# Converting all fourteen weight units of a GLU's second pass during attention, and five first loads of them at once

## The chip, the cores and the metric

The kernel runs on one core of a Trainium2 chip. The metric is the device time of one execution in microseconds (us); lower is better. The engines are named as in the profile: PE (matmuls) with PEld (its weight loads), DVE (VectorE), ACT (ScalarE), POOL (GpSimd) and SP (SyncE, which issues most DMA transfers, in the order of its queue).

## The reference

Random-feature attention over 8 batches, 8 heads, 576 tokens and head dimension 64, with 128 features; its output, as 4608 tokens by 512 features, goes through a gated linear unit with 1536 hidden columns.

```python
def phi(x):                      # x scaled by 64 ** -0.25
    h = einsum('bhsd,md->bhsm', x, omega) - sum(x * x, -1) / 2
    return exp(h - max(h, -1)) / sqrt(m)
q_p, k_p = phi(q_s), phi(k_s)
kv, z = einsum('bhsm,bhsd->bhmd', k_p, v), sum(k_p, 2)
attn = einsum('bhsm,bhmd->bhsd', q_p, kv) / (einsum('bhsm,bhm->bhs', q_p, z)[..., None] + 1e-6)
x = attn.transpose(0, 2, 1, 3).reshape(4608, 512)
out = (1 / (1 + exp(-(x @ w_gate))) * (x @ w_val)) @ w_out
```

The three weight matrices come as 64-bit floats, and the kernel itself turns their bits into 32-bit floats.

## The kernel before, in words

Every product of the gated unit is made of three fp32r matmuls: an operand is split into a high part (a copy on ACT) and a low part (a subtraction on DVE or POOL), and low times high, high times low and high times high are added in PSUM.

**Attention and the first pass.** `attention` is a generator over many small tasks (norms, keys, queries). Its results go to a DRAM tensor `xT`, whose tokens become ready in chunks of 512 (9 chunks). `first_pass` (the generator `gates`) makes 4 of the 12 hidden column tiles for each chunk as soon as its tokens are ready: it loads `xr`, splits it into `xe` (L71, L72), and for each column tile makes a gate and a value product of 12 matmuls (L245) into PSUM. ACT applies Tanh to the gate (`ge`, L266), DVE multiplies (`ye`, L273), SP stores `ye` to DRAM (L278). Each product is one step of `gates`: 8 a chunk, 72 in all. `g` and `y` have two buffers each. The loop that runs attention takes one step of `gates`, then 19 or 11 of attention, and so on until all tokens are ready; what is left of the 72 steps comes after it, when attention's memory (the pool `a`) has been given back to a pool `late`.

**Weights.** The first pass's weights (8 column tiles `wh`, `wl`) are converted at the start. The rest are 14 *units*: eight for the gate and value columns of the second pass, six for the output product. `convert_weights` loads a unit's 64-bit words into a tile (L142, two loads of 512 KB), turns each half into 32-bit floats with six DVE instructions and one on POOL (`from_float64`, L79 to L97), adds four sums of blocks on POOL (L178), and stores the 1 MB result to the DRAM tensor `w32` (L179). It is a generator too: a call issues the loads, a second and a third convert a half each, and the sums and the store come at the beginning of the next call, which goes on to the next unit. Before, 11 units are converted during attention, in two tiles of pool `a` tagged `cv` (the profile's `c`), one call to each step of `gates` from the tenth on (`FROM`); the last 3 (`N_TAIL`) are converted after attention in three of the five `u` buffers of pool `late` (the profile's `late`).

**Units in use.** `unit` loads seven of a unit's eight blocks (L197, L198; 384 and 512 KB) into a `u` tile, and on its second call splits it into high and low parts (L212, L213). There are five `u` buffers in `late` (`UL`) and three in `tail` (`UE`), a pool in the memory that the first pass's weights give back when it is over.

**The second pass** makes the other 8 column tiles: for each of the 9 chunks, `operands` loads `xr` again and makes seven combinations of its blocks (`xl`, `s`; L291, L294, L298), and 8 groups (`gated`) of seven products of six matmuls (L349) follow, group g with unit g. `unit` calls for units not yet split are taken one to a group. The operands of the first chunk are made during the last eight steps of the first pass. Then the output product is made (`last`, L463) and stored.

**Order.** Instructions written with `pin` keep their program order; the others are placed in their engine's queue by a scheduler before the kernel runs. Each engine's queue then runs in order.

Of the kernel before, what the change touches and what calls it, by code (L numbers as in the profile page):

```python
# [14 lines left out]
U32 = mybir.dt.uint32  # L15
# [5 lines left out]
P = 128  # L21
# [14 lines left out]
Q = NC // 2  # L36
# [7 lines left out]
N_LATE = 2 * (NPAIR - EP) + NPAIR  # L44
# [1 line left out]
AT_ONCE = 6  # L46
AHEAD = 8
EVERY = 8
FROM = 10
N_TAIL = 3  # L50
RATE = 11
FIRST = 19

# [4 lines left out]
UL, UE = 5, 3  # L58
# [7 lines left out]
N_OPS = 7  # L66
# [34 lines left out]
def attn_glu_kernel(ctx: ExitStack, tc, qT, kT, qn, kn, va, om, ident, w, out):  # L101
# [610 lines left out]
    def ready(n):  # L712

        return all(through[p] * P >= n for p in range(NP))

    keep = ctx.enter_context(tc.tile_pool(name="keep", bufs=1))
    late = None
    stores = []
    with tc.tile_pool(name="early", bufs=1) as early:
        gates = first_pass()  # L720
        with tc.tile_pool(name="a", bufs=1, side="right") as pool:
            steps = attention(pool)

            def tiles(name):
                return pool.tile([P, 7 * WP], U32, tag="cv", bufs=2, name=name)

            conv = first_weights(early, tiles)
            cycle[:] = ["at", "at", "at", "gv"]
            n = 0
            while not ready(NC):  # L730
                next(steps, None)
                n += 1
                if n % EVERY == 0:
                    next(conv, None)
            cycle.clear()
            later = convert_weights(tiles, range(N_LATE - N_TAIL))
            n = credit = 0
            while not ready(B * S):
                next(gates)
                credit += RATE if n >= 2 * NE - 2 else FIRST  # L740
                while credit >= 1 and not ready(B * S):
                    next(steps, None)
                    credit -= 1
                n += 1
                if next(conv, conv) is conv and n >= FROM:
                    next(later, None)
            for _ in later:
                pass
        late = ctx.enter_context(tc.tile_pool(name="late", bufs=1, side="right"))
        cycle[:] = ["at", "at", "at", "gv"]  # L750

        def tiles(name):
            u = late.tile([P, 2, N_OPS, Q], U32, tag="u", bufs=UL, name=name)
            return u.rearrange("p i n q -> p (i n q)")


        left = 2 * NE * NCH - n
        started, later, parts = [], iter(()), iter(())
        for n, _ in enumerate(gates):
            if n == 2:  # L760
                free = [tiles(f"late{i}") for i in range(N_TAIL)]
                later = convert_weights(lambda name: free.pop(0), range(N_LATE - N_TAIL, N_LATE))
                started = [unit(late, n) for n in range(2)]
                for one in started:
                    next(one)
            elif n in (3, 4):
                next(started[n - 3])
            next(later, None)
            if n == left - 2 * NE:
                parts = operands(0)  # L770
                x = next(parts)
            elif n > left - 2 * NE:
                next(parts, None)
        assert not free and next(later, later) is later
        started = [unit(late, n) for n in range(2, UL)]
        for one in started:
            next(one)

    tail = ctx.enter_context(tc.tile_pool(name="tail", bufs=1))
    started += [unit(tail, n) for n in range(UL, UL + UE)]  # L780
    for one in started[UL - 2 :]:
        next(one)
    next(started.pop(0))
    raws = []
    for c, pair, kind in second_pass(x, parts):
        g = 2 * (pair - EP) + kind
# [99 lines left out]
```

## Time and profile before

| | us |
|---|---|
| median of 3 runs | 1259.02 (1257.65 to 1262.58) |
| the profiled execution's own time | 1265.94 |
| its span, first to last instruction | 1264.1 |
| PE busy | 1199.4 (95% of the span) |
| DVE, ACT, POOL busy | 844.1, 470.4, 425.4 |
| mean granted TensorE clock | 0.961 of full speed |

The profiled execution lies above the three runs; the profile is used for where time goes, the median for the time itself. The stages follow each other roughly so: attention with most of the first pass to about 531 us, the rest of the first pass to about 604, the second pass to about 984, the output product to the end. In a row of the order of time stand the start, the duration, the engine, the line and the operation, and in square brackets the engine's idle time before it and what ended that. A row of windows gives the window, its length, then busy time and count of PE, PEld, DVE, ACT and POOL, the granted clock, the DMA engines' busy share and GB/s.

### The profile page before, as it was taken

How to read it: one execution, taken by the hardware profiler on the slowest of the kernel's cores; microseconds unless marked ns; L12 is line 12 of the kernel's file. 1: busy time of each engine (PE TensorE's matmuls, PEld its weight loads, DVE VectorE, ACT ScalarE, POOL GpSimd, SP SyncE). 2: the span in 40 equal slices, each digit the busy share in tenths (PEclk: the TensorE clock that was granted, in tenths of full speed). 3: DMA queues.
4: the chain of work that ended last, by engine and by line, in shares of the span. 5: the costliest groups of instructions: out<-in, count | busy, mean ns of one | idle time of the engine just before them, and what ended most of it. 6: DMA issues, size and time to landing. Idle time of an engine off the chain costs nothing.

```text
span 1264.1 us, 23448 instructions
## 1 busy us (share of the span) xinstructions
PE 1199.4 (95%) x8956; PEld 1108.8 (88%) x8956; DVE 844.1 (67%) x1838; ACT 470.4 (37%) x963; POOL 425.4 (34%) x435
## 2 busy tenths in 40 slices
PE   5989899999999999999799999999999899999998
PEld 4878778788778787778699999999998899999998
DVE  5654758878777667364866565665668787666774
ACT  3325344445434343230622222322224444333331
POOL 2130010413133122055276666666666211111110
PEclk9978979999989898799799999999999999999999
DMA  8455455668666671265623433233328675666553
GB/s 276 149 173 164 127 165 177 230 217 269 239 201 202 211 243 60 71 231 208 208 88 122 151 122 118 92 122 123 137 83 282 208 219 190 196 192 199 187 184 109
DMA packets 99185, 219.38 MB, mean 174 GB/s; under 512 B 10496, under 2 KB 31232, under 8 KB 97280
## 3 DMA queue, kind: packets, MB, share of 16 engines
q1 hardware_dynamic: 86832, 198.94, 47.6%
q10 hardware_dynamic: 12240, 18.95, 4.1%
q8 instruction: 70, 1.15, 0.4%
q14 instruction: 43, 0.35, 0.1%
HBM read 141.82 MB, written 76.02 MB: 172 GB/s over the span
## 4 chain that ended last, share of the span: by engine, by line
PE 45%; DVE 5%; DMA 3%; issue 1%; SPq 1%; POOL 1%; ACT 0%; DVEq 0%; POOLq 0%; ACTq 0%
PE gw L349 25%; PE po L463 20%; DMA u<-w 1%; DMA xr<-xT 1%; DVE u L213 1%; DMA yr<-ye 1%; POOL late L97 1%; DVE yl L72 0%; DVE late L89 0%; DVE yr L454 0%; DMA ye<-ye 0%; POOL late L178 0%; DVE late L79 0%; DVE late L82 0%; DVE s L298 0%
## 5 line engine op out<-in xcount | busy, mean ns | idle before, releaser
L349 PE MATMUL gw<-xl,u 128*128 128x256 f32 x3024 | 366.0, 283 | 12.3 <-ACT xl L291 4.6
L349 PEld LDWEIGHTS gw<-xl,u 128*128 128x128 f32 x3024 | 363.7, 191 | 14.6 <-ACT xl L291 5.2
L463 PE MATMUL po<-u,yh 128*128 128x256 f32 x1512 | 272.4, 283 | 0.0
L463 PEld LDWEIGHTS po<-u,yh 128*128 128x128 f32 x1512 | 234.8, 191 | 0.0
L463 PE MATMUL po<-u,yl 128*128 128x256 f32 x756 | 214.0, 283 | 4.3 <-DVE yl L72 4.3
L245 PE MATMUL gv<-xe,wh 128*128 128x512 f32 x576 | 194.3, 412 | 1.5 <-POOL xe L72 1.4
L71 ACT ACTIVATE yh<-yr 128x896 fp32r<-128x896 f32 x108 | 99.1, 948 | 159.7 <-DVE yr L454 48.6
L463 PEld LDWEIGHTS po<-u,yl 128*128 128x128 f32 x756 | 144.3, 191 | 4.9 <-DVE yl L72 4.9
L245 PEld LDWEIGHTS gv<-xe,wh 128*128 128x128 f32 x576 | 110.1, 195 | 24.6 <-POOL xe L72 3.6
L245 PE MATMUL gv<-xe,wl 128*128 128x512 f32 x288 | 120.6, 420 | 1.1 <-ACT xe L71 1.1
L72 POOL TENSOR_TENSOR xe<-xr,xe 128x512 fp32r<-128x512 f32 x36 | 48.7, 1371 | 206.5 <-ACT xe L71 203.0
L72 POOL TENSOR_TENSOR yl<-yr,yh 128x896 fp32r<-128x896 f32 x17 | 36.2, 2129 | 218.1 <-ACT yh L71 141.2
L72 DVE TENSOR_TENSOR yl<-yr,yh 128x896 fp32r<-128x896 f32 x91 | 97.2, 1100 | 13.0 <-ACT yh L71 12.0
L594 PE MATMUL pkv<-v,kp 128*128 128x66 f32 x512 | 91.1, 307 | 13.1 <-ACT kp L584 13.1
L594 PEld LDWEIGHTS pkv<-v,kp 128*128 128x128 f32 x512 | 81.3, 221 | 24.0 <-ACT kp L584 17.6
L454 DVE TENSOR_TENSOR yr<-yr 128x128 f32<-128x128 f32 x144 | 60.9, 456 | 60.0 <-DMA yr<-ye 59.5
L329 DVE TENSOR_TENSOR u<-gw,p 128x256 f32<-128x256 f32 x144 | 60.6, 421 | 60.0 <-PE gw L349 50.7
L97 POOL TENSOR_TENSOR c<-c 128x512 f32<-128x512 f32 x22 | 28.1, 1276 | 158.9 <-DVE c L95 88.0
L584 ACT ACTIVATE kp<-ppk,nb 128x128 f32<-128x128 f32 x256 | 69.7, 389 | 30.9 <-DVE nb L575 24.9
L646 PE MATMUL pn<-kv,qp 128*128 128x66 f32 (+1 forms) x640 | 79.4, 279 | 0.0
L646 PEld LDWEIGHTS pn<-kv,qp 128*128 128x128 f32 (+1 forms) x640 | 73.4, 194 | 5.2 <-ACT qp L635 1.9
L635 ACT ACTIVATE qp<-pt 128x512 f32<-128x512 f32 (+1 forms) x80 | 43.6, 554 | 86.8 <-PE pt L633 80.3
(106 smaller groups left out, 1774.6 us busy)
## 6 DMA issues: line engine op xcount, KB each, us to landing
yl<-yl SPq DMA_DIRECT2D x36, 896.0 KB, 3.9
yr<-yl SPq DMA_DIRECT2D x72, 448.0 KB, 4.0
xr<-xT SPq DMA_DIRECT2D x72, 256.0 KB, 4.2
c<-w SPq DMA_DIRECT2D x22, 512.0 KB, 4.6
w<-c SPq DMA_DIRECT2D x11, 1024.0 KB, 4.8
v<-va SPq DMA_DIRECT2D x32, 330.0 KB, 3.7
natk<-kn SPq DMA_DIRECT2D x36, 256.0 KB, 3.6
natq<-qn SPq DMA_DIRECT2D x36, 256.0 KB, 3.3
```

The lines of the kernel that those rows point to most:

```text
L71: nc.scalar.activation(out=hi, in_=x, func=AF.Copy)
L72: (lo_engine or nc.vector).tensor_tensor(out=lo, in0=x, in1=hi.bitcast(F32), op=ALU.subtract)
L97: nc.gpsimd.tensor_tensor(out=x, in0=x, in1=r, op=ALU.add)
L245: nc.tensor.matmul(gv, lhsT=u[:, s], rhs=v, start=(m == 0), stop=(m == 3 * KC - 1))
L329: return nc.vector.tensor_tensor(out=o, in0=a, in1=b, op=ALU.add)
L349: nc.tensor.matmul(o, lhsT=u[:, k, s], rhs=v[:, kc, :], start=(first and m == 0), stop=(m == 5), skip_group_check=not first,)
L454: nc.vector.tensor_tensor(out=raw[:, o], in0=raw[:, a], in1=raw[:, b], op=op)
L463: nc.tensor.matmul(o, lhsT=u[:, i, :], rhs=v[:, k, :], start=(j + m == 0 and n in (1, 6, 5, 4)), stop=(j == NPAIR - 1 and m == 2), skip_gr ...
L584: nc.scalar.activation(out=kp[t, h], in_=pp[:, i, :], func=AF.Exp, bias=nb[:, t - t0, h : h + 1], scale=SCALE,)
L594: nc.tensor.matmul(pkv[:, h, :], lhsT=kp[b * MID + i, h], rhs=v[:, i, h, :], start=(i == 0), stop=(i == MID),)
L635: nc.scalar.activation(out=qp, in_=pt, func=AF.Exp)
L646: nc.tensor.matmul(pn[r, i, :], lhsT=qp[:, i, r], rhs=kvs[u, p, bb][:, h, :], start=True, stop=True,)
```

## The change

All 14 units are converted during attention, in the `cv` tiles, one call to each step of `gates` from the fourth on. After attention no unit is converted: all five `u` buffers of `late` go to units 0 to 4, whose loads are issued together on step 2, and which are split on steps 3, 6, 9, 12 and 15. Units 5 to 7 are loaded when the first pass is over, as before, and split one to a group from the first group on. Before, units 0 and 1 were loaded on step 2 and split on steps 3 and 4, and units 2 to 4 were loaded when the first pass was over.

```diff
@@ -46,8 +46,7 @@
 AT_ONCE = 6
 AHEAD = 8
 EVERY = 8
-FROM = 10
-N_TAIL = 3
+FROM = 4
 RATE = 11
 FIRST = 19
@@ -733,7 +732,7 @@
             cycle.clear()
-            later = convert_weights(tiles, range(N_LATE - N_TAIL))
+            later = convert_weights(tiles, range(N_LATE))
             n = credit = 0
             while not ready(B * S):
                 next(gates)
@@ -749,38 +748,26 @@
         late = ctx.enter_context(tc.tile_pool(name="late", bufs=1, side="right"))
         cycle[:] = ["at", "at", "at", "gv"]
-        def tiles(name):
-            u = late.tile([P, 2, N_OPS, Q], U32, tag="u", bufs=UL, name=name)
-            return u.rearrange("p i n q -> p (i n q)")
-
-
         left = 2 * NE * NCH - n
-        started, later, parts = [], iter(()), iter(())
+        started, parts = [], iter(())
         for n, _ in enumerate(gates):
             if n == 2:
-                free = [tiles(f"late{i}") for i in range(N_TAIL)]
-                later = convert_weights(lambda name: free.pop(0), range(N_LATE - N_TAIL, N_LATE))
-                started = [unit(late, n) for n in range(2)]
+                started = [unit(late, n) for n in range(UL)]
                 for one in started:
                     next(one)
-            elif n in (3, 4):
-                next(started[n - 3])
-            next(later, None)
+            elif started and n % 3 == 0:
+                next(started.pop(0))
             if n == left - 2 * NE:
                 parts = operands(0)
                 x = next(parts)
             elif n > left - 2 * NE:
                 next(parts, None)
-        assert not free and next(later, later) is later
-        started = [unit(late, n) for n in range(2, UL)]
-        for one in started:
-            next(one)
+        assert not started
     tail = ctx.enter_context(tc.tile_pool(name="tail", bufs=1))
-    started += [unit(tail, n) for n in range(UL, UL + UE)]
-    for one in started[UL - 2 :]:
+    started = [unit(tail, n) for n in range(UL, UL + UE)]
+    for one in started:
         next(one)
-    next(started.pop(0))
     raws = []
     for c, pair, kind in second_pass(x, parts):
```

## The prediction

> **What bounds the kernel now.** I read the page first (busy shares, the 40 slices, the chain that ended last), then the windows by stage, then the order of time around the one slice where PE drops.
>
> ```profile
> span 1264.1 us, 23448 instructions
> PE 1199.4 (95%) x8956; PEld 1108.8 (88%) x8956; DVE 844.1 (67%) x1838; ACT 470.4 (37%) x963; POOL 425.4 (34%) x435
> PE   5989899999999999999799999999999899999998
> PEclk9978979999989898799799999999999999999999
> 102.00:194.00 92.00, 85.16 (x624) 72.35 (x624) 53.91 (x144) 42.49 (x124) 5.04 (x4) 0.89 0.50 150
> 194.00:500.00 306.00, 293.34 (x2127) 247.63 (x2125) 231.92 (x592) 135.35 (x353) 82.22 (x83) 0.96 0.62 205
> 500.00:531.00 31.00, 27.95 (x202) 24.25 (x200) 17.87 (x56) 8.60 (x16) 0.00 (x0) 0.85 0.22 82
> 531.00:604.00 73.00, 72.03 (x306) 58.17 (x304) 38.51 (x52) 19.22 (x30) 33.28 (x30) 0.97 0.65 225
> ```
>
> The window rows give length, then busy time (and count) of PE, PEld, DVE, ACT, POOL, then granted clock, DMA share and GB/s. PE is the bound nearly everywhere: 293.34 of 306 us in the middle of attention, 72.03 of 73 in the end of the first pass. A change to DVE and POOL work can only pay where PE waits. The slice string of PE has one clear dip in the middle (the "7", slice 20, 600 to 632 us), and PEclk has its "7" there too. In order of time, PE's own rows there are:
>
> ```profile
> 603.40 0.61 PE L245 MATMUL gv<-xe,wh 128*128 128x512 f32 x2
> 603.95 0.39 PE L349 MATMUL gw<-xl,u 128*128 128x256 f32 x1
> 605.38 0.86 PE L349 MATMUL gw<-xl,u 128*128 128x256 f32 x5 [1.04 <-POOL xl L294]
> 610.87 0.58 PE L349 MATMUL gw<-xl,u 128*128 128x256 f32 x1 [4.64 <-ACT xl L291]
> 613.15 2.72 PE L349 MATMUL gw<-xl,u 128*128 128x256 f32 x11 [1.70 <-DVE xl L294]
> 617.38 15.96 PE L349 MATMUL gw<-xl,u 128*128 128x256 f32 x120 [1.51 <-ACT p L360]
> 608.00:620.00 12.00, 5.92 (x24) 5.33 (x25) 9.62 (x13) 5.33 (x10) 2.87 (x2) 0.50 0.45 135
> ```
>
> The first pass ends at 603.9 (L245) and the second pass (L349) starts haltingly: idle 1.04 + 4.64 + 1.70 + 1.51 = 8.9 us for operands of its first chunk, and half clock (0.50) from 608 to 620. Why the operands are late:
>
> ```profile
> 589.68 0.32 SPq L179 DMA_DIRECT2D w<-late  x1
> 590.10 0.38 SPq L278 DMA_DIRECT2D ye<-ye  x1
> 590.52 2.21 SPq L222 DMA_DIRECT2D xr<-xT  x2
> 593.32 0.50 SPq L197 DMA_DIRECT2D u<-w  x1
> 595.26 0.69 DVE L273 SCALAR_TENSOR_TENSOR ye<-ge,gv 128x512 f32<-128x512 f32 x1 [8.81 <-DMA ye<-ye]
> 599.83 0.85 ACT L212 ACTIVATE u<-u 128x768 fp32r<-128x768 f32 x1 [13.29 <-DMA u<-w]
> ```
>
> SP issues in order. The store of the third late unit (L179) can go only at 589.68, when POOL has finished its sums; behind it stood a store of ye, half of the operand load xr and the loads of units 2 to 4. So DVE waited 8.81 us for a free y, ACT 13.29 us for a unit, and the operands' splits and sums, queued behind those in order, ran until 617. All of it goes back to the three units converted in this stage.
>
> **What the change moves.** Counted from the loops, attention's loop makes 46 of the 72 steps of the first pass (70 attention steps come before; then 19 attention steps to each of the first six, 11 to each later one), which leaves 26; the 306 matmuls of the 531:604 row are 25.5 products of 12, which fits. The generator of the first weights is empty at step 1. Before, calls to the converter fell on steps 10 to 46: 37 calls, and 11 units take 34 (three each and one to end); the last one's store, on step 43, went at 499.31 (last row below). After, they fall on 4 to 46: 43 calls, exactly what 14 units take. Unit i is then loaded on step 4+3i, converted on the next two, summed and stored on 7+3i. Units 2 to 12 get the steps that units 0 to 10 had; new are two units on steps 4 to 10 and one, the last, on 43 to 46.
>
> What a unit costs on each engine (mean ns, x2 halves or x4 sums):
>
> ```profile
> L178 POOL TENSOR_TENSOR c<-c 128x256 f32<-128x256 f32 x44 | 31.3, 731 | 1.7
> L97 POOL TENSOR_TENSOR c<-c 128x512 f32<-128x512 f32 x22 | 28.1, 1276 | 158.9 <-DVE c L95 88.0 <-DVE inv L655 26.4 <-DVE nb L575 13.5
> L89 DVE SCALAR_TENSOR_TENSOR c<-c 128x512 uint32<-128x512 uint32 x22 | 16.0, 727 | 0.2
> L95 DVE SCALAR_TENSOR_TENSOR c<-c 128x512 f32<-128x512 uint32 x22 | 16.0, 726 | 0.1
> L79 DVE TENSOR_SCALAR c<-c 128x512 uint32<-128x512 uint32 x22 | 11.2, 510 | 2.1 <-POOL c L97 2.1
> L82 DVE TENSOR_SCALAR c<-c 128x512 f32<-128x512 f32 x22 | 10.3, 467 | 0.3
> L86 DVE TENSOR_SCALAR c<-c 128x512 uint32<-128x512 uint32 x22 | 9.8, 445 | 0.3
> L93 DVE TENSOR_SCALAR c<-c 128x512 uint32<-128x512 uint32 x22 | 9.7, 440 | 0.0
> 499.31 0.32 SPq L179 DMA_DIRECT2D w<-c  x1
> ```
>
> DVE: 727 + 726 + 510 + 467 + 445 + 440 = 3.3 us a half, 6.6 a unit, 19.9 for three. POOL: 2 x 1.28 + 4 x 0.73 = 5.5 a unit, 16.4 for three. SP: two loads and a store a unit. No matmul is added or taken away.
>
> **Term 1, the stall goes: -13.2 us.** At full speed 2520 matmuls of this form take 300 us (first row below), 0.119 each. The 138 issued from 603.5 to 633.5 would take 16.4 us, and the last L245 ran to 603.86, 0.4 us: 16.8 of 30, so the stall costs 13.2 us, of which 8.9 is idle and 4.3 half clock.
>
> ```profile
> 640.00:940.00 300.00, 300.00 (x2520) 300.00 (x2518) 1.00 0.31 118
> 603.50:633.50 30.00, 20.50 (x138) 19.31 (x138) 0.77 0.54 178
> ```
>
> The second pass has no PE idle of its own in 640:940, and SP, ACT and DVE there do what they did, so what is saved at 604 is still saved at the end. The Trainium skill ("TensorE: Matmul & The Clock Gate", What's actually happening) says that the clock is halved after an idle window of about 3.4 us and comes back after as long a busy one. The 4.64 us gap followed by 0.50 until 620 agrees; by that rule a leftover stall shorter than 3.4 us would cost only itself.
>
> **Term 2, what is late next at 604: +1.5 us.** After the change units 0 to 4 are all loaded at step 2 of the rest and split on steps 3, 6, 9, 12, 15; operands of the first chunk are loaded on step 18 and made on 19 to 25, and nothing stands in SP's way. The products of 26 steps from 530.0 to 603.9 take 2.84 us each, so step 18 is at 581 and the operands have 23 us for seven ACT copies, four sums and seven subtractions. Three of the eight loads that remain (units 5 to 7) need memory that the first pass frees at 603.9; before they were issued after the stall, and now they move to 604. ACT runs in order, and a copy of unit 5 that it meets before the load has landed holds the first groups' copies out of PSUM. The longest such wait for these units before, and the median time from issue to landing:
>
> ```profile
> 624.49 0.85 ACT L212 ACTIVATE u<-u 128x768 fp32r<-128x768 f32 x1 [1.03 <-DMA u<-w]
> u<-w SPq DMA_DIRECT2D x14, 512.0 KB, 6.5
> ```
>
> Bounds 0 and 6.5, a whole landing; I take 1.5, near the wait.
>
> **Term 3, five loads at once: 0.** Ten transfers, 5 x 896 KB = 4.6 MB, from 533.25 on instead of three, then xr of the next chunk.
>
> ```profile
> DMA packets 1601, 4.07 MB, mean 291 GB/s; under 512 B 192, under 2 KB 192, under 8 KB 1600
> 533.25 0.32 SPq L197 DMA_DIRECT2D u<-w  x1
> 536.83 4.49 POOL L72 TENSOR_TENSOR xe<-xr,xe 128x512 fp32r<-128x512 f32 x3 [37.55 <-ACT xe L71]
> ```
>
> The first row is the DMA view for 593 to 607 us, where three such unit loads and part of xr went back to back: 291 GB/s. At that rate five units land by 549.4, and if SP puts this xr (1.05 MB, which cannot go before POOL's split frees its buffer at 541.3) wholly behind them, by 553.0. The next chunk starts on step 10, at 530.0 + 10 x 2.84 = 558.4, and wants its fourth slice 2.1 us into it; the last copy and subtraction take some 2 us. Slack about 5.5 us, so 0. It is gone below 5.65 MB / 25 us = 226 GB/s.
>
> **Term 4, three units inside attention: +2 us.** Below stands what PE itself waits for there.
>
> ```profile
> PE pt L633 <- DVE h L619: 7.6, 8, 1.6
> PE pt L633 <- DVE h L619: 1.9, 2, 1.5
> ```
>
> The first is 194:500 (with conversion), the second 500:531 (without). PE's idle share was 12.7 of 306 us (4%) with conversion, and 6.8 of 92 and 3.1 of 31 (8%) without: by these rows added DVE work shows no price, and it might even be below nothing. The other bound is all of it on the path, 19.9 us. In 102:194 DVE has 38 us free for two units' 13.3, and many tasks run at once. The last unit is the risk: 500:531 is attention's thin end, where h, den, inv and x pass through DVE in turn, and 6.6 us among 56 instructions meets each with 6.6/31 = 21%, for a third of a microsecond or so: 56 x 0.21 x 0.33 = 4 us if each were on the path, and some 1.5 as PE has other products. With 0.5 for the first two units: 2. I take the value near the rows' lower end.
>
> The Trainium skill ("GPSIMD Engine Reference", 1. Specifications) says that GpSimd shares its SBUF interfaces with VectorE, which hurts DVE instructions with two SBUF inputs. The trace agrees:
>
> ```profile
> L89 DVE SCALAR_TENSOR_TENSOR late<-late x6: 687/692/1780, 554.6 to 583.4; 128x512 uint32<-128x512 uint32 x6
> ```
>
> The same instruction took 0.69 to 1.78 us, the longer ones beside POOL work; the mean rows above carry what of it attention shows, and worked through the 16.4 us of POOL it would make term 4 larger by at most as much.
>
> **Sum.** -13.2 + 1.5 + 0 + 2 = -9.7. The profiled execution took 1265.9 with 1.8 us around its span, 0.5% above the median of 1259.0; the stall is no part of that difference, so I take it off the median: 1249.
>
> **The rivals.** 0.5% (6.3 us, 1252.7 and 1265.3) is about what a measurement of this kernel can tell from no change.
> - *The stall is replaced.* Loads at a rate below 226 GB/s (the mean of 531:604 is 225, though with pauses), or ACT held by units 5 to 7 at 604, leave PE idle 4 to 6 us and bring half clock back for as long again at half price: 6 to 9 of 13.2 given back. About 1255. For it: ACT's 13.29 us behind one unit. Against: 291 GB/s while busy, and 5.5 us of slack.
> - *The change does not do what it says.* The first groups stall on the operands of the first chunk whoever is in front, because ye, ge and operands share DVE and ACT with two y buffers: 1259 to 1261. Against: ye went without a wait on DMA except that one of 8.81 us.
> - *Attention pays (slower).* The one place is 500:531: the last unit's sums and store fall on step 46, the units' loads reuse attention's memory and wait for it, and DVE's chain to the last px grows. It is slower from 13.2 + 6.3 = 19.5 us on, which is nearly all 19.9 us of DVE in the path; or less of it, if the half clock of this stage (0.85 now) spreads. About 1267. Against: 38 and 13 us of free DVE in the two windows.
>
> **How the numbers follow.** Stall gone, 0.63: 1249, its own range 1243 (terms 2 and 4 at nothing, and 2 to 3 us of the spread of runs) to 1253. Replaced, 0.20: 1255. Not what it says, 0.08: 1260. Attention pays, 0.09: 1267. Faster: the first case but a twentieth, and a tenth of the second: 0.62. Same: 0.29. Slower: 0.09. The range goes from 1242 to 1260; above it lies the slower case and part of the third, below it little.
>
> **What would show it.** Right: no rows of a late conversion; 28 of each c row on DVE and 14 stores of w32 from c, the last at about 525; ten loads of u together at about 533; PE idle under 3 us and clock near 1.00 from 598 to 630; the slice's 7 gone; then 320 us of L349 as before. Wrong: gv waiting for xe at about 558; L349 waiting for xl or p at 604 with clock 0.50; or first pass and attention ending after 535, with PE waiting for h or x, which would put the loss in term 4.

## The result: slower by 0.9%, and the profile after

The changed kernel took 1272.1 us (median of 6 runs, 1269.2 to 1275.7), the kernel before 1261.9 beside it: 1.0086 of it, with a 95% interval of 1.0059 to 1.0114. The forecast was 1249.0 with a range to 1260. The profiled execution took 1274.9.

Its page, to be held against the rows of before:

```profile
span 1273.1 us, 23455 instructions
PE 1207.0 (95%) x8956; PEld 1115.8 (88%) x8956; DVE 836.3 (66%) x1838; ACT 470.4 (37%) x963; POOL 423.3 (33%) x435
PE   5989889998999999899999999999999899999998
PEclk9998968998999998979999999999999999999999
```

The "7" of PE at 600 us has gone, as forecast. But PE is busy for 7.6 us longer with the same 8956 matmuls, and there are new low digits (the "8"s) at about 160 to 190, 290 to 320 and 510 to 540 us. The mean clock of the whole execution does not tell why: it is 0.966, and 0.961 before. The windows of the stages:

```profile
105.00:207.50 102.50, 94.53 (x619) 80.91 (x619) 58.94 (x156) 41.70 (x119) 10.36 (x10) 0.82 0.47 147
207.50:519.00 311.50, 294.49 (x2144) 248.26 (x2142) 238.30 (x611) 135.04 (x354) 86.22 (x89) 0.96 0.65 217
519.00:551.00 32.00, 25.95 (x180) 22.82 (x181) 22.95 (x61) 8.20 (x15) 5.35 (x6) 0.85 0.22 83
551.00:624.20 73.20, 72.22 (x307) 58.57 (x307) 24.01 (x29) 27.15 (x42) 18.48 (x14) 0.97 0.45 153
623.80:653.80 30.00, 28.63 (x235) 28.19 (x234) 20.16 (x38) 13.68 (x22) 15.86 (x16) 1.00 0.49 175
660.00:960.00 300.00, 300.00 (x2520) 300.00 (x2519) 181.10 (x389) 86.55 (x171) 195.02 (x234) 1.00 0.32 120
```

Attention ends at 551, not 531. From there on the forecast holds: the rest of the first pass takes 73 us as before, the 30 us behind it hold 235 matmuls at full clock (before, 138 of L349 at 0.77), and the second pass is the same 300 us for 2520. In order of time, the boundary is:

```profile
623.53 0.62 PE L244 MATMUL gv<-xe,wh 128*128 128x512 f32 x2
623.99 7.35 PE L348 MATMUL gw<-xl,u 128*128 128x256 f32 x60
632.36 0.98 PE L348 MATMUL gw<-xl,u 128*128 128x256 f32 x6 [1.02 <-ACT p L359]
633.68 26.52 PE L348 MATMUL gw<-xl,u 128*128 128x256 f32 x219 [0.34 <-DVE u L328]
```

1.4 us of idle instead of 8.9. So the loss lies wholly in attention. What PE waited for there, first in the kernel before (102 to 531 us), then after (105 to 551):

```profile
PE pt L633 <- DVE h L619: 12.7, 13, 1.6
PE pkv L594 <- ACT kp L584: 4.7, 7, 1.0
```

```profile
PE pt L632 <- DVE h L618: 16.5, 16, 3.2
PE pkv L593 <- ACT kp L583: 10.6, 8, 3.3
```

(`h` are a query task's scaled scores, made by DVE, and `kp` a key task's exponentials, made by ACT; PE takes both up again.) The longest wait was 1.6 us; now it is 3.3 us, and behind it, as will be seen, the clock is halved.

### The profile page after: what moved, and what is told of

It is laid out like the page before. It is cut to its first block, busy times and chain, and to the rows that moved or that the text cites. A ratio compares the mean times of both kernels' runs of the same rounds, so it can differ in the third digit from the quotient of the medians.

```text
span 1273.1 us, 23455 instructions
## 1 busy us (share of the span) xinstructions
PE 1207.0 (95%) x8956; PEld 1115.8 (88%) x8956; DVE 836.3 (66%) x1838; ACT 470.4 (37%) x963; POOL 423.3 (33%) x435
## 4 chain that ended last, share of the span: by engine, by line
PE 77%; DVE 12%; issue 4%; DMA 4%; POOL 2%; ACT 1%; SPq 0%; DVEq 0%; ACTq 0%; POOLq 0%
PE gw L348 26%; PE po L462 21%; PE gv L244 11%; PE pkv L593 7%; PE pn L645 4%; PE ppk L528 3%; PE ppq L528 2%; PE pt L632 2%; DVE mxq L551 1%; DVE mxk L551 1%; DVE h L618 1%; DMA xr<-xT 1%; PE px L662 1%; POOL c L177 1%; DVE u L212 1%
## 5 line engine op out<-in xcount | busy, mean ns | idle before, releaser
L244 PE MATMUL gv<-xe,wh 128*128 128x512 f32 x576 | 197.6, 418 | 2.2 <-POOL xe L71 2.2
L96 POOL TENSOR_TENSOR c<-c 128x512 f32<-128x512 f32 x28 | 35.7, 1275 | 270.5 <-DVE c L94 117.6
L593 PE MATMUL pkv<-v,kp 128*128 128x66 f32 x512 | 94.5, 313 | 19.0 <-ACT kp L583 19.0
L593 PEld LDWEIGHTS pkv<-v,kp 128*128 128x128 f32 x512 | 85.3, 227 | 30.3 <-ACT kp L583 23.2
L71 DVE TENSOR_TENSOR yl<-yr,yh 128x896 fp32r<-128x896 f32 x91 | 99.6, 1121 | 16.9 <-ACT yh L70 12.0
L645 PE MATMUL pn<-kv,qp 128*128 128x66 f32 (+1 forms) x640 | 83.1, 287 | 0.1
L645 PEld LDWEIGHTS pn<-kv,qp 128*128 128x128 f32 (+1 forms) x640 | 77.1, 201 | 5.6 <-issue 1.3
```

What stands on the lines that cost most here:

```text
L71: (lo_engine or nc.vector).tensor_tensor(out=lo, in0=x, in1=hi.bitcast(F32), op=ALU.subtract)
L244: nc.tensor.matmul(gv, lhsT=u[:, s], rhs=v, start=(m == 0), stop=(m == 3 * KC - 1))
L593: nc.tensor.matmul(pkv[:, h, :], lhsT=kp[b * MID + i, h], rhs=v[:, i, h, :], start=(i == 0), stop=(i == MID),)
L645: nc.tensor.matmul(pn[r, i, :], lhsT=qp[:, i, r], rhs=kvs[u, p, bb][:, h, :], start=True, stop=True,)
```

## The experiments

Ratios are to the kernel before on the same chip, with 95% intervals; "us" is the median. "Tail" is what follows attention.

### Tail or attention?

**e1: the changed kernel's tail alone.** FROM is 10 and 11 units are converted in attention; units 11 to 13 are not (their places get unit 10's words).

```diff
-FROM = 4
+FROM = 10
...
-            later = convert_weights(tiles, range(N_LATE))
+            later = convert_weights(tiles, range(N_LATE - 3))
```

> The end of the first pass as changed (no conversion there, five loads at once), attention as before: 11 units from step 10. Units 11 to 13 are not converted, their places in w32 get unit 10's words. Theory A (the tail gains its 10 to 13 us, and the three more units cost attention 20): 1247 to 1252, and a boundary at 604 with PE idle under 3 us. Theory B (five loads at once or the new order of the tail cost something themselves): 1256 or more.

0.9926 (0.9892 to 0.9959), 1249.9 us. This gains 9.3 us (4 us more or less), about what was forecast for the part after attention, and converting three more units in attention, with all that it brings, costs the difference to 1.0086, some 20 us.

**e2: the early start alone.** The kernel before with FROM = 4; the last units then end on step 37.

```diff
-FROM = 10
+FROM = 4
```

> Before, with the first call to the converter on step 4 instead of 10; still 11 units in attention and 3 after it. Theory A (conversion in attention's thin parts, the wait for the second chunk and the end, lengthens chains and brings half clock): the first two units cost about 10 us in 142 to 207 and the end keeps none, so 1268 to 1272 if what is lost early stays lost, with the stall at the boundary as before. Theory C (it is the number of units, not their place): within 3 us of before, 1259 to 1265.

1.0021 (0.9996 to 1.0046). A small loss at most; but the trace shows it is a balance: at step 36 of the first pass it stands at 437.4 us where e1 stands at 422.5, and it gets most of that back up to step 47, where it has no unit left to convert.

### Which part of a unit's work?

**e3: three units bare.** The changed kernel, in which units 0, 1 and 13 are loaded and a megabyte stored for each, without DVE's and POOL's arithmetic.

```diff
         for h in range(2):
+            if bare:
+                yield
+                continue
             from_float64(
```

> The changed kernel, with units 0, 1 and 13 loaded and stored on their steps but without their DVE and POOL arithmetic (they are stored to a scratch tensor; their places in w32 get a neighbour's words). Theory A: the arithmetic is what costs, so the 20 us of attention mostly go, 1249 to 1255. Theory D (SP's order and the transfers of the added units cost): within 4 us of the changed kernel, 1268 to 1276. If only the order in which the instructions fall changed at random: anywhere between.

0.9916 (0.9884 to 0.9948). Without the arithmetic the whole loss is gone; calls, loads and stores on SP show no price. (But without it the scheduler also leaves attention's instructions nearly in the order of the kernel before, with 22 of PE's 855 rows moved, so that this run alone does not tell the arithmetic from the order; see e16.)

**e5 and e6: one engine's half of it.** e5 leaves out POOL's instructions of those three units, e6 DVE's.

```diff
-    nc.gpsimd.tensor_tensor(out=x, in0=x, in1=r, op=ALU.add)
+    if not bare:
+        nc.gpsimd.tensor_tensor(out=x, in0=x, in1=r, op=ALU.add)
```

> The changed kernel; of units 0, 1 and 13 only the DVE half of the conversion is done (twelve instructions each; POOL's addition and sums are left out, what there is goes to a scratch tensor, their places in w32 get a neighbour's words). Without their arithmetic it was 0.9916 of before, with all of it 1.0086. If DVE's time is the price (19.9 us in a chain that DVE sets): 1.005 to 1.009 of before, some 1267 to 1271. If POOL is the price (it keeps DVE off while it adds): 0.99 to 0.996, 1248 to 1255. Half and half: about 1.000.

> The changed kernel; units 0, 1 and 13 have POOL's work (two additions of the same size, with finite operands from the first weights, and four sums) and none of DVE's. If POOL is the price: 1.005 to 1.009 of before. If DVE's time is the price: 0.99 to 0.996, 1248 to 1255.

e5 1.0006 (0.9979 to 1.0032), e6 0.9938 (0.9906 to 0.9970). Against e3, DVE's 20 us of work go with 0.9%, POOL's 16 us with 0.2%, both together with 1.7%. That does not show that they are worse together: the surplus of 0.6% has an uncertainty as large. Nor does it set DVE's price against POOL's: by their traces e3 and e6 have attention nearly in the order of the kernel before, e5 nearly in that of the changed kernel (1412 and 1318 of attention's matmuls done at the end of step 20), and that order alone costs 0.7% (e17 below). (The profiled execution of e6 lies 10 us above its median, and its times are not used.)

**e7: all of POOL's conversion work on DVE.**

```diff
-    nc.gpsimd.tensor_tensor(out=x, in0=x, in1=r, op=ALU.add)
+    nc.vector.tensor_tensor(out=x, in0=x, in1=r, op=ALU.add)
...
-                nc.gpsimd.tensor_tensor(out=o, in0=x, in1=y, op=ALU.subtract)
+                nc.vector.tensor_tensor(out=o, in0=x, in1=y, op=ALU.subtract)
```

> The changed kernel with POOL's part of the conversion of all units done on DVE: some 3 us more of DVE a unit (0.69 for an addition of 128x512, 0.42 for a sum of 128x256), 42 us in 14 units, and nothing on POOL for it. If POOL's hold on DVE is the price: equal to the changed kernel or up to 15 us faster, 1257 to 1272. If DVE's time is the price: 25 to 40 us slower, 1297 to 1312.

1.0250 (1.0204 to 1.0296), 1293.3 us: 21 us above the changed kernel for 42 us more on DVE, so DVE's work is in good part in the path, though DVE is busy for only 346 of the 473 us from 103 to 576. (The order of attention is another here too.)

### How many units, and where?

**e4: 14 units, none on steps 4 to 9.** FROM is 10, and every fourth step makes two calls.

```diff
-                    next(later, None)
+                    for _ in range(2 if n % 4 == 0 or n == FROM else 1):
+                        next(later, None)
```

> The changed kernel with all 14 units on steps 10 to 43, two calls on every fourth step, so that none is in attention's thin parts. Theory A: the middle takes three units at little cost (DVE 76% to 83%), 1250 to 1256, faster than both kernels. Theory C (each unit costs some 6 us wherever it lies): 1268 to 1274.

1.0036 (1.0007 to 1.0064): 14 us above e1, still most of the loss, in an order of attention of its own.

**e11: the arithmetic of one unit.** Units 1 to 13 are loaded, and their results copied in DRAM from unit 0's.

```diff
-            for _ in converted(cv, NE * WE + n * 4 * Q):
+            for _ in converted(cv, NE * WE + n * 4 * Q, n > 0):
                 yield
+            if n:
+                nc.sync.dma_start(out=w32[n], in_=w32[0])
+                continue
```

> The changed kernel with the arithmetic of unit 0 alone; units 1 to 13 are loaded on their steps but not converted, and their places in w32 are copied from unit 0's. Against the 11 units of the first experiment (0.9926) ten units less of DVE and POOL work. If DVE sets attention's pace at every load: 4 to 7 us a unit, 1183 to 1210, 0.94 to 0.96. If PE is the bound and DVE counts only near the load of 11 to 14 units (as my prediction had it for all): 1235 to 1248, 0.98 to 0.99.

0.9902 (0.9868 to 0.9936), hardly below e1. For a while this looked as if the first eleven units were free. The next run showed that it does not say so.

**e15, e13 and e14: 7, 12 and 13 units.** The changed kernel with FROM = 10, 10 and 7; the units left out get a converted unit's words.

```diff
-FROM = 4
+FROM = 10
...
-            later = convert_weights(tiles, range(N_LATE))
+            later = convert_weights(tiles, range(7))
```

This is e15; e13 has range(12), e14 FROM = 7 and range(13).

> Attention converts units 0 to 6 on steps 10 to 31 (7 units); units 7 to 13 are not converted (their places get the words of unit 6). Else the changed kernel. It repeats the run with the arithmetic of one unit (0.9902) without its copies from memory to memory. Theory M: PE bounds attention below some 11 units, so 4 units less than 0.9926 bring 0 to 4 us: 0.989 to 0.993. If the copies had hidden a gain and DVE work has one price per unit (5 to 7 us, as the last three have): 20 to 28 us less, 0.970 to 0.977, and then the price is no matter of load at all.

> Attention converts units 0 to 11 on steps 10 to 46 (12 units); units 12 and 13 are not converted (their places get the words of unit 11). The stage after attention is that of the changed kernel. With 11 units this stood at 0.9926 of the kernel before, with 14 at 1.0086. Theory M (the price of one more unit rises with the load: nearly nothing up to some 11 units, then the full 6.6 us of DVE and more): the twelfth unit costs 4 to 7 us, ratio 0.996 to 0.999 (1255 to 1258 us). Theory L (it is a matter of place: the unit converted last, in attention's thin end, and the first two in its start pay, the middle ones not): this unit stands in the thin end, so it costs 7 to 10 us, 0.998 to 1.001. Theory A (an average price, the same for each unit, 20 us / 14): 1.4 us, 0.9937.

> Attention converts units 0 to 12 on steps 7 to 46 (13 units); unit 13 is not converted (its place gets the words of unit 12). Else the changed kernel. Theory M: two thirds of the way from 11 units (0.9926) to 14 (1.0086), 1.003, or with a price that still rises 1.001; 1260 to 1263 us. Theory L: the end pays as in the run with 12 units and the first unit of the two in the start pays half of theirs: 1.003 to 1.005. If the step from 12 to 13 is below 2 us and that from 13 to 14 above 8, the first steps (4 to 6) are the place. Theory A: 0.995.

e15 0.9804 (0.9782 to 0.9826), e13 0.9935 (0.9915 to 0.9956), e14 1.0086 (1.0065 to 1.0107). From 7 to 11 units each costs 3.8 us, the twelfth 1 us, the thirteenth 19 us, the fourteenth nothing, each step with some 4 to 5 us of uncertainty (the first, over four units, with 1.3 a unit). The twelfth is the one that ends on step 46, in attention's thin end; the thirteenth is the one that begins on step 7. So no theory of a smooth price holds, neither "nearly free up to 11" nor an average; and the thin end, where the prediction had put the risk, is the cheaper place.

### Load or order?

The traces show something else. Counting matmuls in turn with the same tiles as one row, PE's 855 rows of attention in e1 differ from the kernel before in 1 row and from e13 in 2, but 180 rows of the changed kernel and 161 of e14 stand otherwise. The scheduler had placed attention's own instructions otherwise because of the units added.

**e16 and e17: each load in the other order.** Order edges, which make an engine's queue keep an order and make it wait for nothing, hold attention's PE, ACT and DVE instructions (not the conversions') as they stand in e1 for the changed kernel's work (e16), and as in the changed kernel for e1's work (e17).

```diff
+                for a, b in zip(rank, rank[1:]):
+                    tc.add_manual_dep(of[b], of[a].name, edge, reason="order")
```

> The changed kernel, whole, with attention's matmuls, ACT and DVE instructions (the conversions' own excepted) held by explicit order edges in the order in which the scheduler placed them in the run with 11 units (which is the order of the kernel before). Left to itself, the scheduler placed some 350 of 1397 rows of matmuls in attention otherwise when units are converted on steps 4 to 9. All 14 units are converted, on the same steps. Theory O (the loss is the other order of attention's instructions, not the conversions' time on DVE and POOL): 0.992 to 0.996, 1249 to 1255 us, attention's end at 530 us or before. Theory M (14 units are more DVE work than attention hides, whatever the order): 1.006 to 1.010, no better than the changed kernel; attention's end at 545 to 551. In between by the share of each.

> The run with 11 units from step 10 and the changed kernel's tail (0.9926; units 11 to 13 are not converted), with attention's matmuls, ACT and DVE instructions held by order edges in the order that they have in the changed kernel. Nothing is computed more or less than in that run. Theory O: it loses most of what the changed kernel loses, 1.002 to 1.008, attention's end at 540 to 550 us. Theory M: the order is no matter, 0.991 to 0.995, attention's end at 524 to 530.

| | old order | new order |
|---|---|---|
| 11 units | 0.9926 (e1) | 0.9997, 0.9969 to 1.0025 (e17) |
| 14 units | 1.0065, 1.0036 to 1.0094 (e16) | 1.0086 (the change) |

The new order costs 9 us with 11 units, 3 with 14. The three units cost 17.5 us in the old order, 11 in the new (each of these within some 5 us). So order is a part, the two do not add up, and neither theory was right alone. But e16 and e13 have the same sequence on PE, and can be laid beside each other instruction by instruction. First e13, at the keys of 1_1_0:

```profile
154.98 1.62 DVE L553 TENSOR_REDUCE mxk<-ppk 128x4 f32<-128x512 f32 x3
156.64 0.17 DVE L557 SCALAR_TENSOR_TENSOR hmk<-mxk,sqk 128x10 f32<-128x10 f32 x1
156.84 0.17 DVE L576 SCALAR_TENSOR_TENSOR nb<-sqk,hmk 128x10 f32<-128x10 f32 x1
157.56 2.19 ACT L585 ACTIVATE kp<-ppk,nb 128x128 f32<-128x128 f32 x8
158.00 0.44 PE L595 MATMUL pkv<-v,kp 128*128 128x66 f32 x2 [0.57 <-ACT kp L585]
159.84 1.73 PE L647 MATMUL pn<-kv,qp 128*128 128x66 f32 x14
```

and e16, with unit 0's first half at the same place:

```profile
155.39 0.42 DVE L82 TENSOR_SCALAR c<-c 128x512 uint32<-128x512 uint32 x1
...
156.86 0.68 DVE L555 TENSOR_REDUCE mxk<-ppk 128x4 f32<-128x512 f32 x1
157.46 0.68 DVE L92 SCALAR_TENSOR_TENSOR c<-c 128x512 uint32<-128x512 uint32 x1
158.06 0.68 DVE L555 TENSOR_REDUCE mxk<-ppk 128x4 f32<-128x512 f32 x1
158.66 0.41 DVE L96 TENSOR_SCALAR c<-c 128x512 uint32<-128x512 uint32 x1
158.99 0.42 DVE L555 TENSOR_REDUCE mxk<-ppk 128x2 f32<-128x256 f32 x1
159.33 0.68 DVE L98 SCALAR_TENSOR_TENSOR c<-c 128x512 f32<-128x512 uint32 x1
160.12 1.25 DVE L578 SCALAR_TENSOR_TENSOR nb<-sqk,hmk 128x10 f32<-128x10 f32 x1
160.08 1.26 POOL L100 TENSOR_TENSOR c<-c 128x512 f32<-128x512 f32 x1 [65.82 <-DVE hmk L559]
161.41 2.18 ACT L587 ACTIVATE kp<-ppk,nb 128x128 f32<-128x128 f32 x8 [2.63 <-DVE nb L578]
161.83 0.44 PE L597 MATMUL pkv<-v,kp 128*128 128x66 f32 x2 [3.32 <-ACT kp L587]
165.04 3.19 PE L649 MATMUL pn<-kv,qp 128*128 128x66 f32 x14
```

The c rows, the conversion's, stand between the mxk rows. (A key task is a chain: mxk, the maxima, then hmk and nb, the offset of the exponential, on DVE, then kp, the exponential, on ACT, then pkv, the product, on PE; DVE takes its links in the order of its queue.) And nb, 0.17 us of work, lasts 1.25 us, as long as the POOL sum beside it. The keys come 2.8 us later than in e13 (1.1 of the 3.9 us is e16's later start), PE is idle for 3.32 us, and from then on the same matmuls take almost twice as long (pn 1.73 and 3.19 us). How long that lasts is in the windows, e13 first:

```profile
157.00:162.00 5.00, 4.42 (x40) 4.19 (x38) 1.54 (x7) 3.76 (x13) 0.00 (x0) 1.00 0.26 98
162.00:173.00 11.00, 9.14 (x83) 7.88 (x81) 5.53 (x15) 6.12 (x18) 0.00 (x0) 1.00 0.65 189
173.00:187.00 14.00, 12.98 (x59) 10.30 (x60) 6.11 (x11) 5.23 (x16) 5.04 (x4) 0.52 0.57 181
187.00:200.00 13.00, 13.00 (x102) 11.04 (x101) 11.99 (x28) 5.53 (x10) 0.00 (x0) 1.00 0.47 142
```

```profile
157.00:162.00 5.00, 1.68 (x15) 1.33 (x13) 4.34 (x8) 2.17 (x6) 1.26 (x1) 1.00 0.44 124
162.00:173.00 11.00, 11.00 (x60) 10.81 (x60) 2.29 (x9) 2.87 (x11) 0.00 (x0) 0.51 0.21 71
173.00:187.00 14.00, 13.01 (x60) 10.85 (x56) 7.71 (x18) 6.01 (x18) 4.08 (x5) 0.50 0.33 101
187.00:200.00 13.00, 12.31 (x57) 9.83 (x58) 5.14 (x9) 5.06 (x16) 5.05 (x4) 0.51 0.85 297
```

e13 has half clock for 14 us of this stage, e16 for 38: the place has cost 12 us, the gap among them (step 9 ends at 201.8 instead of 188.6, less the 1.1). The changed kernel has the same gap at 163.9, and others of 3.3 and 3.2 us at 305.9 and 540.9; its three rows, and one of e17:

```profile
163.91 0.70 PE L593 MATMUL pkv<-v,kp 128*128 128x66 f32 x2 [3.31 <-ACT kp L583]
305.93 0.64 PE L593 MATMUL pkv<-v,kp 128*128 128x66 f32 x2 [3.26 <-ACT kp L583]
540.88 0.66 PE L632 MATMUL pt<-id_sb,h 128*128 128x128 f32 x4 [3.23 <-DVE h L618]
```

```profile
293.16 0.70 PE L599 MATMUL pkv<-v,kp 128*128 128x66 f32 x2 [3.68 <-ACT kp L589]
```

Each has a cause of its own. The first comes with a unit on steps 4 to 6: e2, e11, e16 and the changed kernel have it (3.3 us), e5 and e7 too (2.2 and 2.8), and no run without such a unit. e5 has the same rows on DVE there, but no POOL sum beside them, and its nb takes 0.17 us instead of 1.25: that is the 1.1 us by which its gap is shorter.

```profile
160.19 0.17 DVE L580 SCALAR_TENSOR_TENSOR nb<-sqk,hmk 128x10 f32<-128x10 f32 x1
```

The second comes with the order: e17 has it without any added unit, e2 and e5 have it in the new order, e4 and e14 in orders of their own, and no run in the old order does. The third comes with a unit on steps 43 to 46: e13, e14, e16 and the changed kernel have 3.2 to 3.4 us there, e5 2.2.

**e18: the gaps filled.** e16 with 9, 5 and 10 additional matmuls ahead of the three instructions that waited longest, into the same PSUM, which the true ones overwrite.

```diff
+        if (u, p, b) == (1, 1, 0):
+            fill(pkv[:, 0, :], 9)
         for h in range(2):
             for i in range(MID + 1):
                 nc.tensor.matmul(
```

> The run with the changed kernel's work in the old order (1.0065), with PE kept busy in the three longest gaps that its trace shows in attention: ahead of the first pkv of keys 1_1_0 (3.32 us of idle at 161.8, after which the matmuls take nearly twice as long until 199.7), ahead of pt 1_2_0_0 (2.38 us at 209.8) and of pt 3_3_5_0 (3.44 us at 539.7) stand 9, 5 and 10 matmuls more that write the same place of PSUM, which the true ones then overwrite. Everything is computed. Theory G (most of the price of the added units is the half clock that follows a gap of some 3 us where PE's work is sparse, not the gaps and not DVE's time): 0.992 to 0.999, 1250 to 1258 us, attention's end at 528 to 537, clock full from 162 to 173. Theory M (DVE's time on the path of keys and queries): 1.004 to 1.009, attention's end at 545 to 551; PE is busier and nothing ends earlier.

1.0021 (0.9994 to 1.0048), 1262.0 us; attention's end 542. By the ratios that is 5.5 us less than e16 (5 us more or less), with all of DVE's and POOL's work in place and PE busier, between the two theories' numbers. So the gaps with the half clock behind them are a part of the price, though by a margin that is barely clear of the noise. But half clock did not stay away: with a gap of only 1.26 us left, the clock was halved from 163.5 to 173, and again at 400, where e13 has full clock:

```profile
162.00:173.00 11.00, 10.90 (x61) 10.51 (x62) 2.74 (x10) 3.15 (x12) 0.00 (x0) 0.57 0.29 98
173.00:187.00 14.00, 10.52 (x67) 8.39 (x65) 9.70 (x22) 9.21 (x29) 6.57 (x7) 0.87 0.59 195
392.00:400.00 8.00, 7.49 (x68) 6.41 (x66) 6.20 (x13) 4.97 (x14) 4.08 (x5) 0.94 0.46 166
400.00:410.00 10.00, 10.00 (x47) 9.72 (x47) 2.96 (x11) 1.16 (x3) 0.00 (x0) 0.50 0.64 201
```

### The account of attention

A run's attention, from the end of step 4 to that of step 47 of the first pass, can be taken apart: PE idle, plus busy time times (1 - clock), plus matmuls at full clock. The last is 377 to 386 us in all of them.

| run | units | ratio | PE idle | lost to the clock | idle gaps over 1.9 us | order | steps 4 to 15 | 15 to 36 | 36 to 47 |
|---|---|---|---|---|---|---|---|---|---|
| e15 | 7 | 0.9804 | 20.6 | 15.0 | none | old | 135.3 | 182.6 | 94.3 |
| before | 11 | 1 | 22.6 | 28.6 | none | old | 135.3 | 187.0 | 109.0 |
| e1 | 11 | 0.9926 | 22.6 | 20.5 | none | old | 137.1 | 182.2 | 104.8 |
| e3 | 11 and 3 bare | 0.9916 | 23.8 | 20.5 | none | old | 137.4 | 182.7 | 104.7 |
| e13 | 12 | 0.9935 | 25.5 | 23.8 | 3.2 (at 520) | old | 135.3 | 183.8 | 111.2 |
| e16 | 14 | 1.0065 | 30.1 | 39.5 | 3.3, 2.4, 3.4 | old | 156.7 | 182.6 | 110.6 |
| e18 | 14, filled | 1.0021 | 25.6 | 28.8 | none | old | 145.1 | 191.5 | 103.7 |
| e17 | 11 | 0.9997 | 29.6 | 16.9 | 3.7, 1.9 | new | 132.6 | 192.9 | 104.2 |
| e2 | 11, from step 4 | 1.0021 | 25.5 | 25.6 | 3.3, 3.2, 1.9 | new | 142.4 | 192.9 | 93.5 |
| e5 | 14, three on DVE only | 1.0006 | 29.7 | 27.3 | 3.3 and three of 2.2 | new | 141.9 | 195.3 | 101.2 |
| after | 14 | 1.0086 | 31.0 | 37.0 | 3.3, 3.3, 3.2, 1.9 | new | 144.0 | 193.0 | 112.4 |
| e14 | 13 | 1.0086 | 30.4 | 36.6 | 3.2, 3.2, 2.2 | own | 141.6 | 201.0 | 104.6 |
| e4 | 14, steps 10 to 43 | 1.0036 | 31.3 | 27.6 | 3.0 | own | 139.4 | 184.0 | 117.0 |
| e11 | 1 | 0.9902 | 20.4 | 23.9 | 3.3, 2.2 | own | 152.0 | 171.9 | 97.4 |

(The last three columns are the length of three parts of the stretch, in us; "own" is an order that is neither the old nor the new.) From e1 to the changed kernel: 8.4 us of idle and 16.5 us of half clock, 25 in these two profiles (20 by the medians). The idle time is firm, the clock is not: the six profiles with the attention of the kernel before (before, e1, e3, e8, e9, e12) have 22.6 to 23.8 us of idle, but lose 16.6 (e8) to 28.6 us (before) to the clock, 20.9 in the mean; against the profile of the kernel before both terms are 8.4 us. So the clock is some half to two thirds of the price. (In the new order 11 units already have 29.6 us of idle.)

The last columns show where it falls, among runs of one order. From e1 to e16 the first part is 19.6 us longer, the second 0.4, the third 5.8; from e17 to the changed kernel 11.4, 0.1 and 8.2. So the two early units cost 11 to 20 us on the steps where they are converted and just behind them, and nothing later; the last one 6 to 8, though the third part alone differs by up to 8 us between profiles with the same load. The new order costs its time in the second part, 193 to 195 us against 182 to 187 (e18 apart), whatever is converted; the first part of e17 is 4.5 us shorter than that of e1.

The windows of e1 and of after over this stretch say the same of PE's time, 2954 and 2956 matmuls in 401.36 and 418.96 us:

```profile
103.00:527.00 424.00, 401.36 (x2954) 340.13 (x2953) 304.06 (x792) 186.70 (x493) 87.22 (x87) 0.95 0.59 195
```

```profile
103.00:553.00 450.00, 418.96 (x2956) 354.96 (x2956) 321.35 (x831) 186.60 (x493) 101.94 (x105) 0.92 0.58 191
```

e11 explains itself here too: its one unit stands on steps 4 to 6 and makes the gap of 3.3 us at 160.6, so that its first part takes 152.0 us, against 135.3 in e15, and it loses more to the clock than 7 units from step 10 on. (Its copies in DRAM and its order were not tried apart.)

### Versions that leave attention alone

If three units are dear in attention, the other way is to keep them in the tail and take only the stall away.

**e8:** the kernel before, with its late conversions begun on step 0 of the tail, units 0 and 1 loaded on step 10, units 2 to 4 on step 16. **e9:** units 2 to 4 on step 20. **e10:** 10 units in attention and four in the tail. **e12:** e9 with the splits of units 2 to 4 held in the second pass.

```diff
-            if n == 2:
+            if n == 0:
                 free = [tiles(f"late{i}") for i in range(N_TAIL)]
...
+            elif n == 10:
                 started = [unit(late, n) for n in range(2)]
...
+            elif n == 16:
+                started = [unit(late, n) for n in range(2, UL)]
```

That is e8; e9 has 20 for 16, and e12 `unit(late, n, nc.vector)` in the last line.

> The kernel before (11 units in attention, three late) with another order in the end of the first pass: the late conversions from step 0, loads of units 0 and 1 on step 10, splits on 12 and 13, loads of units 2 to 4 on step 16, ahead of the operands' load. If the stall at 604 came from SP's queue, where unit loads and operand load stood behind the last late store at 589.7: the conversions end some 10 us earlier, the stall shrinks to under 4 us and the time is 1248 to 1254, without any price in attention. If the tail simply has too much DVE and POOL work for the operands to be in time: 1257 to 1262.

> As the kernel with the late conversions first (0.9967 of before), but the loads of units 2 to 4 on step 20, behind the operands' load of step 18, and no split ahead of the second pass (unit 2 is split after the first group). What was left of the stall there was the operands' xr, issued at 590 behind unit loads and two stores of ye. If that is so: the first 138 matmuls of the second pass take 18 to 21 us instead of 26.5, and 0.990 to 0.994 of before. If the stall stays, the tail has too little DVE and POOL time for three conversions: 0.996 to 1.000.

> Ten units in attention and four in the tail, late conversions from step 0, each u buffer loaded with a unit when a late conversion has left it (steps 8, 10, 14, 19, 21). If a unit in attention costs 4 to 7 us and the tail has room for a fourth: 2 to 6 us below the kernel with three late units first, 0.988 to 0.994. If the tail has no room: a stall at its end as before or longer, 0.996 to 1.004.

> The kernel before with its three late conversions begun on the first step after attention, loads of units 0 and 1 on step 10, of units 2 to 4 on step 20 behind the operands' load, and the splits of units 2 to 4 held in program order (in the second pass, one to a group) so that ACT does not wait for their loads ahead of the tanh of the first pass. Everything is computed. The run before this one (0.9972) still had 26.8 us for the first 138 matmuls of the second pass where 18.3 would do. If the ACT copies that wait for those loads are what is left of the stall: 18 to 21 us there, 1250 to 1252 us, 0.991 to 0.993. If the loads of u behind the ye stores on SP's queue are: no change, 0.997. Slower than 0.997 if the splits in the second pass now hold its first groups.

e8 0.9967 (0.9944 to 0.9989), e9 0.9972 (0.9946 to 0.9997), e10 1.0008 (0.9981 to 1.0034), e12 0.9977 (0.9959 to 0.9995). e8, e9 and e12 compute everything and cannot be told apart by these intervals; at about 1256.5 us they lie 0.2 to 0.3% below the kernel before, and 1.1 to 1.2% below the changed one. In e8 and e9 the first 138 matmuls of the second pass still take 26.8 us (29.4 before, 18.6 after): SP's stores of ye and loads of u stand in each other's way (argued from its queue, not tried), and ACT, in order, waits for the loads ahead of its tanh, as the first row shows, of e9. e12 takes that wait away (23.6 us there) and meets another, for a sum on DVE that now stands behind the splits (second row, of e12):

```profile
589.02 0.85 ACT L212 ACTIVATE u<-u 128x768 fp32r<-128x768 f32 x1 [4.30 <-DMA u<-w]
```

```profile
PE gw L349 <- DVE u L329: 6.4, 3, 3.6
```

In e10 the gain in attention (its end at 520.5 us) is given back in the tail, where the rest of the first pass takes 87 us instead of 73.

## Why the prediction was wrong

- **Term 1 (-13.2) held.** The first 138 matmuls of the second pass take 18.6 us instead of 29.4, idle 1.4 instead of 8.9, clock 1.00. With terms 2 and 3 the forecast was -11.7; e1 gave -9.3. (Its 603.86 for the end of L245 stands in no row; the last row of L245 ends at 604.01, which moves the sum by 0.15 us.) Its sentence that a leftover stall shorter than 3.4 us would cost only itself is not borne out in attention: there all 24 gaps of 2.2 to 3.7 us in these runs, 22 of them under 3.4, have half clock behind them.
- **Term 2 (+1.5) held:** what is left is a wait of 1.02 us, for ACT, and one of 0.34.
- **Term 3 (0) held, but not in the way forecast.** The ten loads did not go together: three went from 553.30 on, and seven from 563.27 on, behind a store of ye and a load of xr on SP's queue. gv waited for xe once, for 1.0 us, up to the second pass.
- **Term 4 is the step that failed:** +2 forecast, +20 measured (e1 against the change), the upper bound of 19.9. That the two agree is chance: the bound was DVE's time, and the price is idle PE and half clock. Three things in the term were wrong. *"By these rows added DVE work shows no price"* compared PE's idle share in stages that do different work. The same stage with less work was to be had only by a run, and e15 shows a price of 3.8 us a unit, most of it in the last part (94.3 us against 104.8). *"DVE has 38 us free for two units' 13.3"* took free time for cover, but nb, kp and pkv wait for DVE's place in order, not for its share. And the price was reckoned in DVE microseconds, though half to two thirds of it were PE's clock: term 1 had priced half clock behind a gap at 604 (4.3 us), and term 4 did not, though chains already left PE gaps of up to 1.6 us here; at the keys of 1_1_0 an added 2.8 us made 3.3 of 0.6. That added units change the order of attention's own instructions (9 us alone, e17) was in no term.
- **The place was wrong as well.** The prediction put 0.5 us on the two early units and 1.5 on the last one, which it called the risk. By the traces of one order the two early ones cost 11 to 20 us and the last one 6 to 8; by the medians the twelfth unit, at the end, costs 1 us, and the step to a thirteenth, begun on step 7, 19.
- **The rival "attention pays"** was the case that came (1267 against 1272). It named half clock that spreads, but only in 500:531, where the smaller part of the loss lies. With term 2 in the sum it was slower from 18.0 us on, not from 19.5, and at 0.09 its chance was far too small for a term whose two ends were 0 and 19.9.

Shown: three more units cost some 17 us with attention's order held (e16 against e1), the early units make the first gap and the new order the second, and gaps with half clock behind them are a part of the price (e16, e18). Not shown: DVE's share of the whole price against POOL's. Not settled: how much of the rest is order. The scheduler's order changes with the units added, and e17 loses 9 us by it alone though its profile, at the quick end of its runs, has 7 us more idle than e1 and no more lost clock. Nor was it found what halves the clock where no gap is long.

## What to carry to other kernels

Where PE's work is sparse and chained, an off-path engine's free time is no cover: look for the chain that passes through its queue, add the new instructions to the longest gap that PE already has there, and ask whether it passes some 2 us. In attention of these runs each of the 24 gaps of 2.2 us or more had half clock within 2 us of its end, for 3.4 us or more at a time, and four of the seven gaps of 1.9 to 2.15 us had it; at the keys of 1_1_0 a gap of 3.3 us cost 12 us in all. (Half clock came without such a gap as well.) Before dividing a price among parts, see whether the scheduler kept the order of the rest. And a price read from another stage of the same profile is a bound at best; give the whole span between the bounds its chance.

## What the hardware showed unexpectedly

- A DVE instruction of 0.17 us with two SBUF inputs (nb) lasted 1.25 us, to the end of the POOL tensor_tensor of 1.26 us that ran beside it. The Trainium skill ("GPSIMD Engine Reference", 1. Specifications) says that GpSimd shares its SBUF interfaces with VectorE, to the cost of DVE instructions with two SBUF inputs; the row agrees, and gives the size here: the whole POOL instruction. Without it beside (e5), nb took 0.17 us at the same place.
- The Trainium skill ("TensorE: Matmul & The Clock Gate", What's actually happening) lets the clock come back after some 3.4 us of sustained work. The rows of e16 do not agree: in 162:173 PE was busy for 11.00 of 11.00 us at 0.51, and half clock lasted until 199.7. In e18 it came behind a gap of 1.26 us, and at 400 after a stretch with 7.49 of 8 us busy and no gap over 1.9. So PE's busy time, as the profile shows it, does not foretell the clock in these runs.
